# One reciprocal-square-root table function in place of Ln and Exp, in front of a kept Newton step

## The chip, the cores and the metric

The kernel runs on one core of one Trainium2 chip. The metric is device time in microseconds (us) of one execution. The core has a matrix engine (PE in the profile, with its weight loads as PEld), a vector engine (DVE), an activation engine (ACT), GpSimd (POOL), and SyncE (SP), which issues most DMA transfers. Each engine works through its own instructions in a fixed order and waits on semaphores for the others.

## The reference

Three stages stand behind each other: a linear attention with a root-mean-square norm, and two MLPs with different activations.

```
kv  = einsum('bhsd,bhse->bhde', k, v)
out = einsum('bhsd,bhde->bhse', q, kv)
rms = sqrt(mean(out * out, axis=-1) + 1e-06)
x   = out / rms * g_norm                      # 8 batches, 8 heads, 576 x 64 each
h = x @ w_in1;  g = where(h >= 1, h, where(h <= -1, 0, (h + 1)**2 / 4));  x = g @ w_out1
h = x @ w_in2;  g = max(h, 0)**2;                                         out = g @ w_out2
```

There are 4608 tokens, the model width is 512, and the hidden width of each MLP is 2048. Weights arrive as 64-bit floats and are read as pairs of 32-bit words.

## The kernel before, in words

Every fp32 product of the MLPs is made from three matmuls on pieces: each operand is split into a rounded upper piece (a CAST on ACT, line 217) and the remainder (a subtraction on DVE, lines 185, 230 and 807). The tokens are worked through in blocks of 512. Blocks of the first MLP are plain (`h_stage`, `g_stage`, `out_stage`, the matmuls of line 238); later work goes in pairs of blocks with fewer products (line 878).

The attention of batch 0 comes first, by four pairs of heads hp = 0 to 3 (`t_first`, `o_first`, `r_first`), with fillers on PE (`keep_warm`, matmuls on a tile of zeros, line 1157) between them. The attention of the other seven batches (`t_stage`, `o_stage`, `r_stage`) is spread as hooks over the steps of the block before. Beside the first attention the weights are narrowed and split (`split_w`: a Prelu on ACT in line 268, two DVE operations in lines 270 and 271, a CAST and a subtraction).

For one pair of heads the norm does this. PE multiplies q and kv into `po` (two halves of 288 columns), ACT squares each half into `y` (line 512) and scales it into `o` (line 209; DVE does the second half in line 211), PE averages the squares over a head with a matrix of ones into `pr` (line 534). Then comes the inverse root: ACT takes Ln of each half (line 535), Exp of both halves at once (line 537) and the square of the result into `t` (line 224, reached from line 538). DVE makes the Newton step: `newton` multiplies `t` by `pr` plus 1e-6 (line 519, once for each half), `norm` adds -3 and multiplies by `y` (line 522) and then by `o` (line 523). The result is split into the upper and lower piece of `x`, on which the first MLP's matmuls wait. In `r_stage` the same statements stand in lines 602, 604 and 606.

The eight PSUM banks are handed out in a ring during the first attention. So `pr` of pair 1 takes the bank of `pr` of pair 0, and has to wait until DVE's line 519 has read that; and a group of three fillers takes the bank of `pkv` of pair 2, and has to wait until DVE has copied that (line 219). A scheduler puts the instructions of each engine in order by its own estimates of their durations and by priorities; the program's text gives only dependencies and a rough order.

Of the kernel before, what the change touches and what calls it, by code (L numbers as in the profile page):

```python
# [10 lines left out]
F32 = mybir.dt.float32  # L11
F32R = mybir.dt.float32r
AF = mybir.ActivationFunctionType
ALU = mybir.AluOpType
I32 = mybir.dt.int32
BF16 = mybir.dt.bfloat16

LN_SCALE = 2.0**-44  # L20
LN2 = 0.6931471805599453

# [51 lines left out]
def linear_attention_rms_two_mlps(  # L78
# [12 lines left out]
    nc = tc.nc  # L91
# [3 lines left out]
    P = 128  # L95
# [17 lines left out]
    const = ctx.enter_context(tc.tile_pool(name="const", bufs=1))  # L113
# [73 lines left out]
    ident = ap2.tile([P, P], F32, tag="q", name="ident")  # L187
    ones = const.tile([P, P], F32R, name="ones")
    gvec = const.tile([P, 1], F32, name="gvec")
    lnb = const.tile([P, 1], F32, name="lnb")  # L190
    expb = const.tile([P, 1], F32, name="expb")
    halfb = const.tile([P, 1], F32, name="halfb")
    kv0 = wp.tile([P, NP, P], F32, tag=f"w1_{NF - 1}", name="kv0")
    rests = [const.tile([P, 2, 2, D], F32, name=f"rest{i}") for i in range(2)]
# [9 lines left out]
    def engine(op, phase):  # L204
        return engines[next(turns[op][min(phase, 2)])]
# [16 lines left out]
    def square(e, dst, src):  # L222
        if e is nc.scalar:
            e.activation(dst, src, AF.Square)  # L224
        else:
            e.tensor_tensor(dst, src, src, ALU.mult)

    def split(t, src, op, phase):
        hi = copy(engine(op + "_hi", phase), t[:, 0, :], src)
        lo = engine(op + "_lo", phase).tensor_tensor(  # L230
            t[:, 1, :], src, t[:, 0, :].bitcast(F32), ALU.subtract
        )
        return hi, lo
# [162 lines left out]
    def bank(b, name):  # L396

        pool, tag = next(banks) if b == 0 else (ps_t, "at")
        return pool.tile([P, TB], F32, tag=tag, name=name)

    def scratch(hp, kind):

        which, f = {"y": (0, 12), "o": (0, 8), "t": (1, 11), "qT": (1, 7)}[kind]
        return wp.tile([P, 2, U], F32, tag=f"w{which}_{f + hp}", name=f"{kind}_0_{hp}")
# [36 lines left out]
    def load_first():  # L441


        left = wp.tile([REM, 2, H, D], F32, tag="w0_7", name="kvr0")
        qr = wp.tile([REM, H, D], F32, tag="w1_6", name="qr0")
        for hp in range(NP):
            load_kv(0, hp)
            heads = slice(2 * hp, 2 * hp + 2)
            kvr[0, hp] = (left[:, 0, heads, :], left[:, 1, heads, :])
            pool, tag = (ep, "e") if hp == NP - 1 else (st, "st")  # L450
            t = pool.tile([P, TB], F32, tag=tag, name=f"q_0_{hp}")
            t = t.rearrange("p (c h d) -> p c h d", h=2, c=MR)
            rows = q[0, 2 * hp : 2 * hp + 2, :TB, :].rearrange("h (p c) d -> p c h d", p=P)
            nc.sync.dma_start(t, rows)
            qs[0, hp] = [t[:, c] for c in range(MR)] + [qr[:, heads, :]]
            if hp == 1:
                for f in range(2):
                    load_w(1, f, 0)
            if hp == 0:
                for d, src in ((left[:, 0], k), (left[:, 1], v), (qr, q)):  # L460
                    nc.scalar.dma_start(d, src[0, :, TB:, :].rearrange("h p d -> p h d"))
                for j in range(2):
                    nc.scalar.dma_start(
                        gvec[j * D : (j + 1) * D, :], g_norm.rearrange("(d o) -> d o", o=1)
                    )
# [52 lines left out]
    def newton(t, m):  # L518
        nc.vector.scalar_tensor_tensor(t, m, 1e-6, t, op0=ALU.add, op1=ALU.mult)  # L519

    def norm(t, y, o):
        nc.vector.scalar_tensor_tensor(t, t, -3.0, y, op0=ALU.add, op1=ALU.mult)  # L522
        nc.vector.tensor_tensor(t, o, t, ALU.mult)
# [3 lines left out]
    def r_first(hp):  # L527
        y, o = og.pop((0, hp))
        t = scratch(hp, "t")
        ms = []  # L530
        for half in range(2):
            ps = bank(0, f"pr_0_{hp}_{half}")
            m = ps[:, :U]
            nc.tensor.matmul(m, ones.bitcast(F32), y[:, half], start=True, stop=True)  # L534
            nc.scalar.activation(y[:, half], m, AF.Ln, bias=lnb, scale=LN_SCALE)
            ms.append(m)
        nc.scalar.activation(y, y, AF.Exp, bias=expb, scale=-0.5)
        square(engine("y", 0), t, y)
        for half in range(2):
            newton(t[:, half], ms[half])  # L540
        norm(t, y, o)
        n = TB // 2
        rem = xrem[0][:, hp, :].rearrange("p (h r) -> p h r", h=2)
        nc.gpsimd.tensor_copy(rem, t[:, :, n:])
        x = xs[1, 0][hp].rearrange("p a (h n) -> p a h n", h=2)
        marks.append(split(x, t[:, :, :n], "x", 0))
# [42 lines left out]
    def r_stage(b, hp):  # L589
        (y, o), _ = hl.pop((b, hp))  # L590
        if (b, hp) in WHOLE:
            products = [(ones.bitcast(F32), y)]
        else:
            products = [(ones, s2) for s2 in og.pop((b, hp))]
        ms = []
        for half in range(2):
            c = slice(half * U, (half + 1) * U)
            ps = bank(b, f"pr_{b}_{hp}_{half}")
            m = ps[:, :U]
            for n, (one, s2) in enumerate(products):  # L600
                nc.tensor.matmul(m, one, s2[:, c], start=n == 0, stop=n == len(products) - 1)  # L601
            nc.scalar.activation(y[:, c], m, AF.Ln, bias=lnb, scale=LN_SCALE)
            ms.append((c, m))
        nc.scalar.activation(y, y, AF.Exp, bias=expb, scale=-0.5)
        t = ap1.tile([P, S], F32, tag="wk2", name=f"t_{b}_{hp}")
        square(engine("y", b), t, y)
        for c, m in ms:
            newton(t[:, c], m)
        if b < LAST_B:
            norm(t, y, o)  # L610
            nc.gpsimd.tensor_copy(xrem[b][:, hp, :], t[:, TB:])
            split(xs[1, b][hp], t[:, :TB], "x", b)
            return
        xt = st.tile([P, TB], F32, tag="st", name=f"xt_{hp}")
        nc.vector.scalar_tensor_tensor(t, t, -3.0, y, op0=ALU.add, op1=ALU.mult)
        nc.vector.tensor_tensor(xt, o[:, :TB], t[:, :TB], ALU.mult)
        nc.vector.tensor_tensor(xrem[b][:, hp, :], o[:, TB:], t[:, TB:], ALU.mult)
        x_kept[hp] = xt
# [17 lines left out]
    def attention_first():  # L636

        slots = {}

        def at(s, f, *a):  # L640
            slots.setdefault(s, []).append((f, a))

        at(0, begin, 0)
        for hp in range(NP):
            at(6 * hp, kv_stage, 0, hp)
            at(6 * hp, t_first, hp)
            at(6 * hp + 8, o_first, hp)
            at(6 * hp + 13, r_first, hp)
        return slots

    def attention(b, base, every, order):

        slots = []
        for j, hp in enumerate(order):
            s = base + every * j
            turn.setdefault((b, hp), len(turn))
            if b == 1:
                slots += [(max(0, s - 7), load_kv, b, hp), (s, kv_stage, b, hp)]
            elif j % 2 == 0:
                two = order[j : j + 2]  # L660
                turn[b, two[1]] = len(turn)
                slots += [(max(0, s - 7), load_kv, b, i) for i in two]
                slots.append((s, kv_stage, b, *two))
            slots += [
                (max(0, s - 7), load_q, b, hp),
                (s, t_stage, b, hp),
                (s + 3, o_stage, b, hp, 0),
                (s + 4, o_stage, b, hp, 1),
            ]
            if j == 0:  # L670
                slots.append((s + 6, begin, b))
            slots.append((s + 6, r_stage, b, hp))
            if b == LAST_B:
                slots.append((s + 8, keep_x, b, hp))
        if b < LAST_B:
            slots.append((2 * NF * b, store_xrem, b))
        return slots
# [465 lines left out]
    for i, t in enumerate((7, 9, 11, 13, 15, 21, 23)):  # L1143
        hook(last + t, load_w2)

    nc.scalar.preload_act_table_set("natural_log_exp_and_others")
    load_first()
    for f, w in ((2, 0), (3, 0), (0, 1), (4, 0), (1, 1), (5, 0), (2, 1), (6, 0), (3, 1)):
        load_w(1, f, w)
# [18 lines left out]
        nc.gpsimd.memset(t, 0.0)  # L1168
    nc.gpsimd.memset(kv0, 0.0)
    nc.vector.tensor_scalar_mul(gvec, gvec, -0.5)  # L1170
    nc.vector.memset(lnb, LN_SCALE * 1e-6)
    nc.vector.memset(expb, -22.0 * LN2)
    nc.vector.memset(halfb, 0.5)

    kvw = ap1.tile([P, 2, P], F32, tag="hl1", name="kvw")
# [10 lines left out]
    for s in sorted(first):  # L1186
        for f, a in first[s]:
            if f in (o_first, r_first):
                with tc.high_priority():
                    f(*a)  # L1190
            else:
                f(*a)
# [102 lines left out]
```

## Time and profile before

| | us |
|---|---|
| median of 3 runs | 1556.57 (1556.27 to 1558.22) |
| the profiled execution's own time | 1556.74 |
| span of its instructions | 1554.7 |
| ACT busy in the span | 909.6 |
| DVE busy in the span | 1131.3 |

The profiled execution is 0.17 us above the median, and 2.04 us of it lie outside the span. The granted TensorE clock reads 1.00 over the span.

### The profile page before, as it was taken

To read this page: it belongs to the slowest core of one execution; us is meant where nothing else is said; L and a number is where in the kernel's file an instruction comes from. 1 tells how busy PE (TensorE), PEld (TensorE's weight loads), DVE (VectorE), ACT (ScalarE), POOL (GpSimd) and SP (SyncE) were. 2 spreads that over 40 slices of the span, in tenths; PEclk is the share of its full clock that TensorE was granted. 3 is DMA by queue.
4 is the path that set the end of the run, shared out by engine and by line. 5 is a ranking of instruction groups with operands and counts; after the bars stand their busy time and mean duration, and the time that the engine had idled before them with its cause. 6 is when DMAs were issued, how large, how long until landed. Compare 5 with 4: busy or idle time off the path is not lost.

```text
span 1554.7 us, 22267 instructions
## 1 busy us (share of the span) xinstructions
PE 1545.8 (99%) x7727; PEld 1283.3 (83%) x7729; DVE 1131.3 (73%) x2000; ACT 909.6 (59%) x1713; POOL 20.5 (1%) x38
## 2 busy tenths in 40 slices
PE   9999999999999999999999999999999999999999
PEld 5787888888888888888888888888888888888898
DVE  6986886877877776754587559778965596558666
ACT  5977766767666676664355346456644463446354
POOL 0000000000000000000000000000000000000000
PEclk9999999999999999999999999999999999999999
DMA  9666899996877967935676867696876676877796
GB/s 288 197 216 187 278 319 279 304 313 197 274 250 238 284 208 227 293 98 172 193 245 194 227 213 246 197 238 200 259 227 204 205 238 197 241 248 224 212 392 249
DMA packets 327519, 368.22 MB, mean 237 GB/s; under 512 B 196976, under 2 KB 222576, under 8 KB 327408
## 3 DMA queue, kind: packets, MB, share of 16 engines
q1 hardware_dynamic: 295360, 308.60, 66.4%
q10 hardware_dynamic: 32048, 58.20, 9.9%
q8 instruction: 61, 1.00, 0.3%
q14 instruction: 50, 0.41, 0.1%
HBM read 282.59 MB, written 84.15 MB: 236 GB/s over the span
## 4 chain that ended last, share of the span: by engine, by line
PE 97%; ACT 1%; DVE 1%; issue 0%; DVEq 0%; ACTq 0%
PE po L878 27%; PE ph L878 27%; PE acc L238 20%; PE ph L238 19%; PE pkv L479 1%; PE po L238 1%; PE pr L601 1%; PE pwarm L1157 1%; ACT raw L268 0%; ACT w L217 0%; PE pr L534 0%; DVE t L519 0%; DVE w L185 0%; PE po L511 0%; DVE t L522 0%; PE po L569 0%
## 5 line engine op out<-in xcount | busy, mean ns | idle before, releaser
L878 PE MATMUL ph<-x,ws 128*128 128x512 f32 (+1 forms) x2016 | 422.4, 371 | 0.0
L878 PEld LDWEIGHTS ph<-x,ws 128*128 128x128 f32 x2016 | 355.8, 188 | 65.6
L878 PE MATMUL po<-t,ws 128*128 128x512 f32 x1680 | 381.6, 389 | 0.0
L878 PEld LDWEIGHTS po<-t,ws 128*128 128x128 f32 x1680 | 315.3, 188 | 65.5
L238 PE MATMUL ph<-x,w 128*128 128x512 f32 x1344 | 329.4, 392 | 1.3 <-ACT w L217 0.6
L238 PEld LDWEIGHTS ph<-x,w 128*128 128x128 f32 x1344 | 248.7, 188 | 54.3 <-ACT w L217 1.5
L807 DVE TENSOR_TENSOR t<-g,t 128x512 fp32r<-128x512 f32 (+1 forms) x288 | 183.3, 641 | 92.2 <-ACT t L217 84.6
L217 ACT CAST t<-g 128x512 fp32r<-128x512 f32 (+1 forms) x288 | 166.5, 585 | 101.8 <-PE po L878 50.2
L238 PE MATMUL acc<-gs,w 128*128 128x512 f32 x696 | 173.0, 392 | 1.5 <-DVE u L707 1.5
L238 PE MATMUL acc<-gs,wt 128*128 128x512 f32 x648 | 157.9, 391 | 0.0
L238 PEld LDWEIGHTS acc<-gs,w 128*128 128x128 f32 x696 | 128.6, 188 | 27.8 <-DVE u L707 1.9
L949 ACT ACTIVATE g<-h 128x512 f32<-128x512 f32 (+1 forms) x120 | 70.7, 589 | 119.8 <-DVE h L938 119.8
L238 PEld LDWEIGHTS acc<-gs,wt 128*128 128x128 f32 x648 | 120.1, 188 | 24.3
L705 ACT ACTIVATE u<-ph,halfb 128x512 f32<-128x512 f32 x112 | 77.2, 690 | 91.5 <-PE ph L238 89.1
L938 DVE CUSTOM_DVE_ANT_0 h<-ph,e 128x512 f32<-128x512 f32 (+1 forms) x120 | 76.4, 638 | 64.8 <-PE ph L878 57.3
L707 DVE SCALAR_TENSOR_TENSOR u<-u,ph 128x512 f32<-128x512 f32 x112 | 76.3, 681 | 54.2 <-ACT u L224 53.8
L928 DVE TENSOR_TENSOR e<-ph,e 128x512 f32<-128x512 f32 (+1 forms) x96 | 61.1, 643 | 50.2 <-PE ph L878 49.6
L230 DVE TENSOR_TENSOR gs<-u,gs 128x512 fp32r<-128x512 f32 x112 | 76.8, 686 | 22.2 <-ACT gs L217 21.8
L217 ACT CAST gs<-u 128x512 fp32r<-128x512 f32 x112 | 69.7, 622 | 37.5 <-DVE u L707 34.7
L224 ACT ACTIVATE u<-u 128x512 f32<-128x512 f32 x112 | 70.8, 632 | 1.4 <-ACT u L705 0.5
L217 ACT CAST x<-xr 128x512 fp32r<-128x512 f32 (+1 forms) x84 | 49.0, 586 | 36.0 <-DVE xr L858 17.5
L807 DVE TENSOR_TENSOR x<-xr,x 128x512 fp32r<-128x512 f32 (+1 forms) x84 | 53.1, 637 | 7.3 <-ACT x L217 7.3
(134 smaller groups left out, 1494.5 us busy)
## 6 DMA issues: line engine op xcount, KB each, us to landing
ws<-wsd SPq DMA_DIRECT2D x336, 512.0 KB, 4.2
wsd<-s ACTq DMA_DIRECT2D x96, 512.0 KB, 4.7
wt<-wsd SPq DMA_DIRECT2D x54, 512.0 KB, 5.4
raw<-in_moe_w_in_dram SPq DMA_DIRECT2D x32, 512.0 KB, 5.8
raw<-in_moe_w_out_dram SPq DMA_DIRECT2D x32, 512.0 KB, 6.2
xr<-x1d SPq DMA_DIRECT2D x36, 256.0 KB, 4.9
out_dram<-ov SPq DMA_DIRECT2D x142, 64.0 KB, 3.5
wsd<-w SPq DMA_DIRECT2D x17, 512.0 KB, 5.0
```

Source lines behind the costliest of these rows:

```text
L217: return e.copy(dst, src)
L224: e.activation(dst, src, AF.Square)
L230: lo = engine(op + "_lo", phase).tensor_tensor(t[:, 1, :], src, t[:, 0, :].bitcast(F32), ALU.subtract)
L238: nc.tensor.matmul(dst, wt(a), xt(c), start=first and n == 0, stop=last and n == 2)
L479: nc.tensor.matmul(ps[s, d], lhs, rhs, start=c == 0, stop=c == MR)
L705: nc.scalar.activation(u, ps, AF.Relu, bias=halfb, scale=0.5)
L707: nc.vector.scalar_tensor_tensor(u, u, 1.0, ps, op0=ALU.min, op1=ALU.max)
L807: engine2(op + "_lo").tensor_tensor(t[:, 1, :], src, t[:, 0, :].bitcast(F32), ALU.subtract)
L878: nc.tensor.matmul(ps, wt(a), xt(c), start=first and n == 0 and i == 0, stop=last and n == len(lhs) - 1 and i == 2, skip_group_check=True,)
L928: nc.vector.tensor_tensor(e[i, p], bank, e[i, 1], ALU.add)
L938: nc.vector._custom_dve(TENSOR_ADD_SAT, out=h, in0=bank, in1=add, s0=float("inf"), s1=0.0)
L949: nc.scalar.activation(g, h, AF.Square)
```

## The change

The two Ln activations and the Exp of a pair become two activations with the function Abs_reciprocal_sqrt, which write `y` directly; the constant tiles for Ln and Exp go, one for 1e-6 comes, and the table set that is loaded at the start is another. The square, the Newton step and all that follows stay. There are 32 pairs, 4 in `r_first` and 28 in `r_stage`.

```
-LN_SCALE = 2.0**-44
-LN2 = 0.6931471805599453
...
-    lnb = const.tile([P, 1], F32, name="lnb")
-    expb = const.tile([P, 1], F32, name="expb")
+    epsb = const.tile([P, 1], F32, name="epsb")
...
-            nc.scalar.activation(y[:, half], m, AF.Ln, bias=lnb, scale=LN_SCALE)
+            nc.scalar.activation(y[:, half], m, AF.Abs_reciprocal_sqrt, bias=epsb)
             ms.append(m)
-        nc.scalar.activation(y, y, AF.Exp, bias=expb, scale=-0.5)
         square(engine("y", 0), t, y)
...
-            nc.scalar.activation(y[:, c], m, AF.Ln, bias=lnb, scale=LN_SCALE)
+            nc.scalar.activation(y[:, c], m, AF.Abs_reciprocal_sqrt, bias=epsb)
             ms.append((c, m))
-        nc.scalar.activation(y, y, AF.Exp, bias=expb, scale=-0.5)
...
-    nc.scalar.preload_act_table_set("natural_log_exp_and_others")
+    nc.scalar.preload_act_table_set("abs_reciprocal_sqrt_and_small")
...
-    nc.vector.memset(lnb, LN_SCALE * 1e-6)
-    nc.vector.memset(expb, -22.0 * LN2)
+    nc.vector.memset(epsb, 1e-6)
```

The scheduler answers with another order on ACT, DVE, PE and SP, from the first pair of heads on. Lines of the changed kernel are 7 to 11 smaller than those before; the names with numbers are tiles, and the first number behind `y`, `o`, `t`, `pr`, `po` and `pkv` is the pair of heads.

ACT, first attention, from the mean squares of pair 0 to the square into `t` of pair 0, before:

```order
L535 ACTIVATE y_0_282<-pr_0_0_333,lnb 128x288
L268 ACTIVATE raw_0_0_151<-raw_0_0_151 128x512
L535 ACTIVATE y_0_282<-pr_0_1_336,lnb 128x288
L537 ACTIVATE y_0_282<-y_0_282,expb 128x576
L512 ACTIVATE y_1_348<-po_1_0_350 128x288
L209 ACTIVATE o_1_349<-po_1_0_350,gvec 128x288
L512 ACTIVATE y_1_348<-po_1_1_354 128x288
L224 ACTIVATE t_0_332<-y_0_282 128x576
L217 CAST w_0_0_300<-d_0_0_297 128x2x256
L268 ACTIVATE raw_0_1_153<-raw_0_1_153 128x512
```

ACT at the same place, of the changed kernel:

```order
L527 ACTIVATE y_0_280<-pr_0_0_331,epsb 128x288
L260 ACTIVATE raw_0_0_150<-raw_0_0_150 128x512
L527 ACTIVATE y_0_280<-pr_0_1_334,epsb 128x288
L216 ACTIVATE t_0_330<-y_0_280 128x576
L260 ACTIVATE raw_0_1_152<-raw_0_1_152 128x512
L504 ACTIVATE y_1_345<-po_1_0_347 128x288
L201 ACTIVATE o_1_346<-po_1_0_347,gvec 128x288
L504 ACTIVATE y_1_345<-po_1_1_351 128x288
L209 CAST w_0_0_298<-d_0_0_295 128x2x256
```

The Exp is gone, the square into `t` of pair 0 has moved ahead of the three instructions of pair 1, and so has the Prelu on `raw_0_1`, whose input comes by DMA.

DVE, first attention, from the Newton step of pair 0 to the first copies of pair 2 (`kv` and `qT`, which PE reads for `po` of pair 2), before:

```order
L519 SCALAR_TENSOR_TENSOR t_0_332<-pr_0_0_333,t_0_332 128x288
L519 SCALAR_TENSOR_TENSOR t_0_332<-pr_0_1_336,t_0_332 128x288
L185 TENSOR_TENSOR w_0_0_300<-d_0_0_297,w_0_0_300 128x2x256
L522 SCALAR_TENSOR_TENSOR t_0_332<-t_0_332,y_0_282 128x576
L271 SCALAR_TENSOR_TENSOR d_0_1_363<-raw_0_1_153,d_0_1_363 128x512
L523 TENSOR_TENSOR t_0_332<-o_0_283,t_0_332 128x576
L219 COPY kv_126<-pkv_2_303 64x64 x2
L219 COPY qT_2_316<-pt_2_0_317 128x288
L519 SCALAR_TENSOR_TENSOR t_1_393<-pr_1_0_394,t_1_393 128x288
```

DVE, of the changed kernel, from the Newton step of pair 1 (that of pair 0 stands seven rows ahead of it, directly behind line 263 on `d_0_0`):

```order
L511 SCALAR_TENSOR_TENSOR t_1_390<-pr_1_0_391,t_1_390 128x288
L511 SCALAR_TENSOR_TENSOR t_1_390<-pr_1_1_394,t_1_390 128x288
L222 TENSOR_TENSOR x_0_0_215<-t_0_330,x_0_0_215 128x512
L514 SCALAR_TENSOR_TENSOR t_1_390<-t_1_390,y_1_345 128x576
L211 COPY kv_125<-pkv_2_301 64x64
L515 TENSOR_TENSOR t_1_390<-o_1_346,t_1_390 128x576
L211 COPY kv_125<-pkv_2_301 64x64
L211 COPY qT_2_314<-pt_2_0_315 128x288
L211 COPY qT_2_314<-pt_2_1_320 128x288
L222 TENSOR_TENSOR x_0_1_216<-t_1_390,x_0_1_216 128x512
```

The copies of pair 2 stood ahead of the Newton step of pair 1 and now stand behind it. On PE, one of the four fillers ahead of `pr` of pair 1 stands behind it now, `po` of both halves of pair 2 stands together now, behind five fillers, and so does `pr` of pair 2; before, `pr` of its second half stood behind the first two matmuls of the MLP. POOL's order is the same, and SP's too through the first attention; later some loads of weights, q and k change places on SP by a few rows.

## Rows read from the trace of the kernel before

**Rows 1.** The page, busy time of each engine in the span.
```profile
PE 1545.8 (99%) x7727; PEld 1283.3 (83%) x7729; DVE 1131.3 (73%) x2000; ACT 909.6 (59%) x1713; POOL 20.5 (1%) x38
```
**Rows 2.** Waits of PE, whole span: us in total, times, longest.
```profile
PE acc L238 <- DVE u L707: 1.5, 1, 1.5
...
PE pr L534 <- DVE t L519: 0.9, 1, 0.9
PE ph L238 <- ACT w L217: 0.6, 2, 0.4
PE ph L238 <- DVE kv L219: 0.4, 1, 0.4
```
**Rows 3.** Busy time in two stretches: PE, PEld, DVE, ACT, POOL; clock, DMA, GB/s.
```profile
40.00:60.00 20.00, 18.05 (x91) 13.22 (x90) 18.76 (x35) 19.66 (x40) 0.00 (x0) 1.00 0.95 274
60.00:1550.00 1490.00, 1489.82 (x7422) 1247.07 (x7421) 1084.52 (x1899) 867.03 (x1630) 16.83 (x24) 1.00 0.76 236
```
**Rows 4.** Timeline of PE: start us, us, instruction, idle before it.
```profile
1.19 4.73 PE L1157 MATMUL pwarm<-warm 128*128 128x512 bf16 x11 [1.19 <-DVE warm L1152]
...
17.82 1.24 PE L534 MATMUL pr<-y,ones 128*128 128x288 f32 x4 [0.91 <-DVE t L519]
...
32.30 13.03 PE L238 MATMUL ph<-x,w 128*128 128x512 f32 x56 [0.28 <-DVE t L519]
...
49.00 3.33 PE L238 MATMUL ph<-x,w 128*128 128x512 f32 x12 [0.44 <-ACT w L217]
53.84 0.97 PE L238 MATMUL acc<-gs,w 128*128 128x512 f32 x3 [1.51 <-DVE u L707]
...
57.33 4.27 PE L238 MATMUL acc<-gs,w 128*128 128x512 f32 x17
```
**Rows 5.** Instructions of ACT by form: count, busy us, mean ns, idle before.
```profile
L604 ACT ACTIVATE wk<-wk,expb 128x576 f32<-128x576 f32 x28 | 22.0, 785 | 0.3
...
L535 ACT ACTIVATE y<-pr,lnb 128x288 f32<-128x288 f32 x8 | 3.9, 501 | 3.7 <-PE pr L534 3.7
```
**Rows 6.** Timeline of ACT, start and first attention.
```profile
0.73 1.28 ACT L1146 ACT_TABLE_LOAD   x1 [0.73 <-PEq L1273]
...
14.43 0.78 ACT L537 ACTIVATE y<-y,expb 128x576 f32<-128x576 f32 x1
...
16.58 0.69 ACT L224 ACTIVATE t<-y 128x576 f32<-128x576 f32 x1
17.16 0.63 ACT L217 CAST w<-d 128x512 fp32r<-128x512 f32 x1
17.66 0.69 ACT L268 ACTIVATE raw<-raw 128x512 f32<-128x512 f32 x1
...
20.82 0.68 ACT L224 ACTIVATE t<-y 128x576 f32<-128x576 f32 x1
...
31.07 0.69 ACT L224 ACTIVATE t<-y 128x576 f32<-128x576 f32 x1
```
**Rows 7.** Timeline of DVE, first attention and the steps behind it.
```profile
15.34 0.42 DVE L270 TENSOR_SCALAR d<-raw 128x512 int32<-128x512 int32 x1
...
17.31 0.82 DVE L519 SCALAR_TENSOR_TENSOR t<-pr,t 128x288 f32<-128x288 f32 x2
...
19.92 0.75 DVE L523 TENSOR_TENSOR t<-o,t 128x576 f32<-128x576 f32 x1
20.59 0.45 DVE L219 COPY kv<-pkv 64x64 f32<-64x64 f32 x2
...
39.34 0.68 DVE L230 TENSOR_TENSOR x<-t,x 128x512 fp32r<-128x512 f32 x1
...
53.11 0.68 DVE L707 SCALAR_TENSOR_TENSOR u<-u,ph 128x512 f32<-128x512 f32 x1
```
**Rows 8.** Timeline of SP's queue: the issue of the first weight loads.
```profile
7.35 0.93 SPq L250 DMA_DIRECT2D raw<-in_moe_w_in_dram  x2
```
**Rows 9.** The weight tiles raw up to 62 us: time from issue to landing.
```profile
DMA to landing us min/median/max: 4.4/8.1/11.2
```

## The prediction

> **What bounds the kernel now.** I read the page's engine totals first: PE is busy for 1545.8 of 1554.7 us, ACT for 909.6, DVE for 1131.3 [rows 1]. A gain on ACT alone is therefore worth something only where PE waits for ACT or for what hangs on it. The second view, the list of PE's waits, says how little that is: apart from its first start, PE waits in five places of the whole program, for 1.5, 0.9, 0.6 and 0.4 us [rows 2] and the 0.28 that stands at 32.30 [rows 4], 3.7 us together. The third, busy time by stretches, says where: from 60 to 1550 us PE is busy for 1489.82 of 1490 us, while ACT has 867.03 us of work there, so that 28 of the 32 removed Exps come out of time in which ACT has room; from 40 to 60 us ACT (19.66 of 20) and DVE (18.76) are full and PE is not (18.05) [rows 3]. The fourth, PE's timeline, gives the places: 0.91 us at 16.9 before `pr` of pair 1, 0.28 at 32.0, 0.44 at 48.6, and 1.51 at 52.3 before the first `acc` [rows 4]. Behind that PE hardly waits again. So the change is worth what it moves the first 58 us, and the rest shifts with it.
>
> **What goes.** Per pair of heads, one Exp of 0.78 us, 28 of them in the later batches [rows 5, 6]. A queued instruction starts about 0.1 us before the one ahead ends (the square at 16.58 lasts 0.69, the CAST behind it starts at 17.16 [rows 6]), so the Exp holds ACT's queue for 0.68 us, 4 x 0.68 = 2.7 us in the first attention. The 28 others lie beside PE work; that cover goes only if ACT becomes full again, and the change makes it emptier.
>
> **What comes.** The new function has no row. The nearest is the Ln it replaces, with the same operands (PSUM source, a tile as bias, 128x288): 0.501 us [rows 5]. I take that, so 0. Below it could lie 0.4, if it cost as little as 0.1 less per half; above it the Exp's 0.78 on twice the columns, 0.28 more per half, 0.56 per pair. With the upper end four pairs lose 2.2 us on ACT, nearly all that the Exp gives.
>
> **What moves, place by place.** I laid the rows of the new order behind each other from 13 us on, each with the duration of the same instruction before, less the overlap of 0.1 us; I give the points that decide.
>
> At 14 us: the second root of pair 0 ends near 14.4, where the Exp starts now [rows 6], and the square into `t` follows at once, ahead of pair 1: 14.4 instead of 16.58. DVE's two Newton instructions move up into the place that line 270 has now, 15.34 instead of 17.31 [rows 6, 7]. That frees the bank for which `pr` of pair 1 waits. The next limit is pair 1's own squares. Their way is longer by the Prelu on `raw_0_1`, which now stands ahead of them and holds ACT until about 15.8; the squares then end at 16.2 and 16.9. PE, with three fillers in place of four after `po`, reaches `pr` at 16.6 and goes on without a wait: 1.2 us before the 17.82 of now [rows 4]. The square into `t` of pair 1 comes at 18.4 instead of 20.82 [rows 6].
>
> At 20 us the new order gives some back. The copies of `kv` of pair 2 run at 20.59 now [rows 7]; in the new order they stand behind pair 1's Newton pair (19.1 to 19.85), a split (0.60) and lines 522 and 523 (0.67 each, as from 19.92 to 20.59), and end at 22.2 with their own 0.45 [rows 7]. PE, done with the transposes at 20.0 and with three fillers at 20.6, meets a filler that needs this bank: a new wait of about 1.6 us, with nothing on PE to hide it, since all that is queued behind it waits too: `po` and `pr` of pair 2, and all of pair 3. Behind it `po` of pair 2 runs whole, so both halves of `pr` come at 26.6 and 27.2, and the square into `t` of pair 2 at 29.0 instead of 31.07 [rows 6]. PE has done by 31.3 what it has done by 32.30 now, the small wait there included [rows 4]: 1.0 us ahead, while ACT and DVE are 2 us ahead.
>
> From 31 to 51 us: the last split of `x` comes on DVE at 37.3 instead of 39.34 [rows 7]. PE is covered until then by matmuls on the first three pieces, as now. Then DVE and ACT are full [rows 3]. DVE goes through 24 rows from there to line 707 of step 2, the one that frees the bank of the first `acc`; 7 of them line 270 at 0.34 us, 17 others at 0.60, and three waits for CASTs of 0.5 together, that is 13.1 us from 37.9 on, so line 707 starts at 51.0 instead of 53.11 [rows 7], and `acc` at 51.7 instead of 53.84 [rows 4]. PE gets there at 51.6: of its lead of 1.0 it first loses some at the weights of step 6 (`ph`, at 49.00 now, [rows 4]), whose upper piece I place at 48.4 and whose lower piece at 49.3; the wait of 1.51 is turned into two of 0.8 and 0.5.
>
> From there to 57.7 the order differs by a few matmuls; counted by matmuls done, 0.1 to 0.2 us more is gained. Sum: -2.1 and -0.1, **2.2 us earlier**, and PE has no later wait to give it back. On SP nothing is moved past another within the first attention; the loads that change places later are covered by PE's run from 60 to 1550 us [rows 3], and if one should come late, that is a new stall of case E. 1556.74 - 2.2 = 1554.5 for an execution like the profiled one, which is 0.17 above the median: **1554.4 us**.
>
> A rule of the Trainium skill speaks against the change. The trace shows the load of a table once, 1.28 us at the start [rows 6], and the order of the changed kernel holds one too. The Trainium skill, "ScalarE: Activation LUTs", section "Table sets: the hidden batching unit", says that a function outside the active set needs a load of its set first, and prices a switch at about 2.66 us. If Square, Prelu or Relu were not in the new set, that would be an estimate of 8 switches on the way of the first four pairs, 21 us by that page; the single load in the order speaks against it.
>
> **Rivals.** (B) The gain does not arrive, about 1556.6. It would be so if the stretch from 31 to 57 us, where DVE is full, began no earlier: if the new function costs the upper bound, or the wait at 20.6 us is 2 us longer than I place it. For it: DVE's 18.76 of 20, and that one place gives back 1.6 us already. Against it: ACT's chain of pair 2 comes out 2 us early even with that wait.
>
> (C) More than forecast, about 1553.0: the new wait at 20.6 is short, the lower piece of step 6's weights is in time, and PE keeps 3.5 us. The waits that exist add up to 3.7, and the 12 matmuls at 49.00 take 0.6 more than at the pace of the 56 at 32.30, 0.23 us each [rows 4]; 4.3 less, 1552.3, is the floor.
>
> (D) Slower than before, about 1558.7: the Prelu on `raw_0_1` now stands ahead of pair 1 on ACT, and waits for a DMA. Its load is the second of the two issued from 7.35, done by 8.3 [rows 8]; these loads land 4.4 to 11.2 us after issue [rows 9]. Each microsecond past 15.2 delays all behind it; from 17.4 on the gain is gone, and at 8.3 + 11.2 = 19.5 it costs 4.3 - 2.2 = 2.1 us. Against it: line 270 of now reads this tile at 15.34 [rows 7], so it had landed.
>
> (E) The loads of tables come back, in ACT's chain of the first attention: two a pair, by the row of the load [rows 6] 8 x 1.28 - 2.2 = 8 us more, 1564.6; or some load on SP holds up a block. The order's single load speaks against the first, the work that covers PE against the second.
>
> The clock is no case of its own: the eleven fillers from 1.19 us on take 0.43 us each, 512 columns at the lower of the two levels (1.2 GHz), while after the wait of 1.51 us at 52.3 the 17 matmuls at 57.33 take 0.25 each, the upper one [rows 4]; the new wait is as long as that one.
>
> **Chances.** Forecast 0.60, own range 1553.3 to 1555.6; B 0.15; C 0.15; D 0.06; E, with any other new stall in the reordered steps, 0.04. What this measurement tells from no change is about 0.2%, 3.1 us, so from 1553.46 down it is faster and from 1559.68 up slower. Faster: C and 0.05 of the forecast, 0.20. Slower: E and half of D, 0.07. The rest, 0.73, is within. The range goes from 1552.6, just under C, to 1557.8, over B and the milder part of D.
>
> **What would show it.** In the changed profile: line 537 gone and one table load; the new function at 0.50 us; the square into `t` of pair 0 near 14.4 and of pair 2 near 29; PE's wait before `pr` of pair 1 gone, a wait of 1 to 2 us at a filler near 20.6 in its place; `acc` first at 51 to 52.5; no wait of PE between 60 and 1550 us; ACT busy for some 25 us less in all. A wait of PE after 60 us, or an `acc` at 53.8 or later, would make the forecast wrong; so would a Prelu that waits for its DMA at 15 us.

## The result and the profile after

| | before | after |
|---|---|---|
| median of 6 runs, us | 1556.79 (1556.27 to 1558.81) | 1565.95 (1564.18 to 1568.39) |
| after / before, 95% interval | | 1.0057 (1.0045 to 1.0070) |
| profiled execution: own time, span, us | 1556.74, 1554.7 | 1568.35, 1566.6 |

The change makes the kernel 0.57% slower, some 9 us. The forecast was 1554.4 us, and the range ended at 1557.8. One execution of the thirteenth run below (2274.56 us, mean granted clock 0.635) and one of the kernel before (1937.68 us, 0.746) are left out of every comparison.

In the changed kernel the lines are 7 to 11 lower: the new function is line 527 (535 before) and 593 (602), a matmul of the MLPs 230 (238), a CAST 209 (217), `u` 697 (707), Newton 511, 514 and 515 (519, 522, 523), `qf` and `qT` 549 and 551 (558, 560), `wf` 333 (341).

The engine totals, which answer to [rows 1]:

```profile
PE 1550.2 (99%) x7729; PEld 1285.1 (82%) x7729; DVE 1129.9 (72%) x1999; ACT 888.8 (57%) x1681; POOL 14.6 (1%) x38
```

ACT has lost 20.8 us of work, and PE has gained 4.4 with the same matmuls (two records of them are missing in the trace before). Then the waits of PE, against [rows 2]: engine, what waits, what it waits for, us in total, times, longest.

```profile
PE po L230 <- ACT qT L209: 3.4, 3, 2.5
PE ph L230 <- DVE u L697: 3.1, 2, 1.6
PE pwarm L1147 <- DVE kv L211: 1.5, 1, 1.5
PE ph L230 <- ACT w L209: 1.3, 1, 1.3
...
PE pr L592 <- ACT wk L201: 1.0, 1, 1.0
PE pkv L471 <- DMA v<-in_v_dram: 0.8, 2, 0.6
```

PE's timeline, against [rows 4], puts them in their places:

```profile
23.31 0.80 PE L1147 MATMUL pwarm<-warm 128*128 128x512 bf16 x2 [1.51 <-DVE kv L211]
...
51.18 3.37 PE L230 MATMUL ph<-x,w 128*128 128x512 f32 x12 [1.31 <-ACT w L209]
54.48 1.91 PE L230 MATMUL acc<-gs,w 128*128 128x512 f32 x7
...
120.82 0.40 PE L592 MATMUL pr<-s,ones 128*128 128x288 f32 x1 [0.97 <-ACT wk L201]
132.14 3.02 PE L230 MATMUL ph<-x,w 128*128 128x512 f32 x12 [1.61 <-DVE u L697]
...
209.93 0.40 PE L230 MATMUL po<-qT,kvbd 128*128 128x288 f32 x1 [0.45 <-ACT qT L209]
321.46 3.01 PE L230 MATMUL ph<-x,w 128*128 128x512 f32 x12 [1.53 <-DVE u L697]
500.80 0.40 PE L230 MATMUL po<-qT,kvbd 128*128 128x288 f32 x1 [0.47 <-ACT qT L209]
556.18 0.61 PE L230 MATMUL po<-qT,kvbd 128*128 128x288 f32 x1 [2.51 <-ACT qT L209]
```

Six waits stand where the kernel before had one of 0.18 us [rows 3]: 0.97 + 1.61 + 0.45 + 1.53 + 0.47 + 2.51 = 7.5 us. The busy times by stretches say the same, and show the clock (the column behind POOL):

```profile
22.00:24.00 2.00, 0.69 (x3) 0.30 (x3) 1.94 (x6) 0.62 (x1) 0.24 (x1) 0.89 1.11 359
24.00:26.00 2.00, 2.00 (x6) 1.12 (x5) 1.31 (x3) 0.80 (x2) 0.00 (x0) 0.50 1.04 373
26.00:28.00 2.00, 2.00 (x25) 1.25 (x23) 0.85 (x3) 1.88 (x4) 0.00 (x0) 0.76 1.05 384
...
60.00:1550.00 1490.00, 1482.19 (x7327) 1236.53 (x7326) 1077.62 (x1884) 845.64 (x1594) 11.22 (x24) 1.00 0.77 235
556.00:562.00 6.00, 5.82 (x21) 4.94 (x22) 3.45 (x7) 3.85 (x11) 0.00 (x0) 0.72 0.86 225
```

From 60 to 1550 us PE is busy 7.6 us less than before. At the waits that end at 23.31 and 556.18 us the granted clock is 0.89, 0.50 and 0.76 in three stretches and 0.72 in the last, down at the lower of its two levels (1.2 GHz of 2.4) for all or part of them. Worked out from these rows, that costs PE (0.11 + 0.50 + 0.24) x 2 + 0.28 x 6 = 3.4 us, most of its 4.4 us more of busy time. Where the last 1.0 comes from is not shown; it need not be the clock, since in the profile of the tenth run below PE is busy for 1548.0 us, 2.2 more than before, with a clock of 1.00 from 60 to 1550 us. The account of the two profiled spans closes: 7.4 us more of waits behind 60 us and 4.4 more of busy time make 11.8 of the 11.9 us. The waits of the first 60 us, first start included, add up to 4.8 us in both.

The six executions fit this. The two with a mean granted clock of 1.000 took 1564.2 and 1564.3 us, 7.5 above the kernel before, as much as the six waits; the other four, at 0.998 and 0.999, took 1566.0 to 1568.4.

Where the waits come from is read on DVE's timeline. This is the step ahead of the longest:

```profile
546.59 0.69 DVE L333 TENSOR_TENSOR wf<-wf 128x512 f32<-128x512 f32 x1 [3.36 <-DMA wf<-wsd]
547.20 0.68 DVE L697 SCALAR_TENSOR_TENSOR u<-u,ph 128x512 f32<-128x512 f32 x1
...
549.39 0.81 DVE L511 SCALAR_TENSOR_TENSOR t<-pr,t 128x288 f32<-128x288 f32 x2
...
554.16 0.77 DVE L549 STREAM_TRANSPOSE qf<-q 128x576 f32<-128x576 f32 x1
```

DVE stands 3.36 us for the transfer of `wf`, a weight tile that is being prepared for later steps. Behind it in the queue stand `u` (an activation of an MLP), a Newton step and `qf` (a transposed q); ACT makes `qT` from `qf`, and PE waits 2.51 us for `qT`. In the kernel before, this Newton step (537.46 us) and `qf` (542.87) were done before DVE came to `wf` (558.16).

### The profile page after: what moved, and what is told of

It is laid out like the page before. It is cut to its first block, busy times and chain, and to the rows that moved or that the text cites. A ratio compares the mean times of both kernels' runs of the same rounds, so it can differ in the third digit from the quotient of the medians.

```text
span 1566.6 us, 22236 instructions
## 1 busy us (share of the span) xinstructions
PE 1550.2 (99%) x7729; PEld 1285.1 (82%) x7729; DVE 1129.9 (72%) x1999; ACT 888.8 (57%) x1681; POOL 14.6 (1%) x38
## 4 chain that ended last, share of the span: by engine, by line
PE 66%; DMA 1%; DVE 1%; ACT 0%; issue 0%; SPq 0%; DVEq 0%
PE po L868 27%; PE ph L868 27%; PE acc L230 6%; PE ph L230 5%; PE po L230 0%; DMA wf<-wsd 0%; DMA x1d<-ev 0%; PE pkv L471 0%; PE pr L592 0%; ACT qT L209 0%; DVE gs L222 0%; DVE u L697 0%; ACT s L209 0%; DVE t L515 0%; DVE t L511 0%
```

## The experiments

Theory (order): the list scheduler, given 32 instructions less, wrote another order for every engine; some instructions that wait for a transfer, or weights that have time, now stand in front of steps that PE needs. The order moved 164 of PE's 7385 instructions, 357 of ACT's 1811, 419 of DVE's 1999 and 49 of SP's 940. Rival (function): the reciprocal square root, its table, or the Newton step behind it costs the time. The addresses came in as a second rival after the first four runs.

Where an order is pinned, each engine's instructions get edges that fix their order and nothing else, from a table:

```diff
+ORDER = {"PE": ..., "Activation": ..., "DVE": ..., "SP": ..., "Pool": ...}
...
+        for a, b in zip(order, order[1:]):
+            tc.add_manual_dep(b, a.name, ..., reason="order")
...
         linear_attention_rms_two_mlps(tc, *args)
+        pin_order(tc)
```

Ratios are to the kernel before, in runs on the same chip, with 95% intervals.

### Order or function: four runs

The first puts a do-nothing operation where the Exp stood, so that the scheduler writes the old order (in both places):

```diff
+        nc.scalar.activation(y, y, AF.Identity, bias=zerob, scale=1.0)
```

> The kernel after with one more ACT operation (Identity, y to y, at both places where Exp stood). All work of the kernel after is in it, and every engine has its instructions in the order of the kernel before. Order theory (the loss of the kernel after is the new order that the scheduler gave all engines when the Exp went): within 1.5 us of the kernel before, about 1556.7 us, and the PE waits of the kernel after behind 60 us (120.8, 132.1, 209.9, 321.5, 556.2 us, some 7.5 us together) are gone. Function theory (the reciprocal square root itself, its table or what it leaves to the Newton step costs the time): as the kernel after, 1564 to 1568 us, with the same waits.

Measured: 1557.70 us, ratio 1.0000 (0.9991 to 1.0009). From 60 to 1550 us PE has one wait of 0.18 and one of 0.24 and is as busy as before [rows 3] (PE alone; then clock, DMA, GB/s):

```profile
60.00:1550.00 1490.00, 1489.58 (x7414) 1.00 0.77 236
```

The second takes the Exp out of the kernel before (in both places), which gives the new order without the new function:

```diff
-        nc.scalar.activation(y, y, AF.Exp, bias=expb, scale=-0.5)
```

> The kernel before with the Exp left out (the Newton step is given the logarithm, so the output is not the reference's): Ln stays, no new function, and the order of all engines is that of the kernel after. Order theory: as the kernel after, 1564 to 1568 us, with PE waits near 121, 132, 210, 321, 500 and 556 us. Function theory: no slower than the kernel before, 1552 to 1557 us.

Measured: 1566.61 us, 1.0059 (1.0046 to 1.0071), as the kernel after. Its waits of PE:

```profile
PE po L238 <- ACT qT L217: 5.0, 3, 2.8
PE ph L238 <- DVE u L705: 2.3, 2, 1.6
```

They stand at 118.8, 130.1, 210.3, 322.1, 502.1 and 556.7 us, the places of the kernel after. These two runs settle it: the function is innocent, the order is not. Both keep two constants, and with them the addresses of the kernel before, so the second rival does not touch this reading.

The third is the new function in the old order, pinned; the fourth pins the new order up to 61.7 us and the old one behind it.

> The kernel after, with the order of every engine's instructions pinned to that of the kernel before without the Exp. Order theory: the gain that the prediction saw in the first 60 us and nothing lost behind it, 1553.5 to 1557 us, no PE wait above 0.5 us behind 60 us, the filler's wait of 1.5 us at 22 us gone and the old one at 52 us back. Function theory: 1564 to 1568 us. A third reading (in before's order the gain of the first stage is taken back at the next wait anyway, since the pace of the start is set by transfers) gives 1556 to 1557 us, the same as before.

> The kernel after with the order pinned: its own order up to the second projection of the block at 61.7 us, and from there the order of the kernel before. Theory: the first attention alone costs at most 2.5 us (0.5 us that PE is behind at 58 us, and up to 1.7 us where the clock falls behind the filler's wait), so 1556 to 1559 us; the rest of the loss (5 to 9 us) is in the order behind 61.7 us. Rival: what is lost was laid in the first attention, with the later waits as its echo: 1563 us or more.

Measured: 1560.12 us, 1.0015 (1.0006 to 1.0023), and 1560.82, 1.0018 (1.0009 to 1.0027). The fourth is 0.7 us above the third, with intervals that overlap, so the new order of the first attention loses little; the great part lies behind it. But both miss their ranges. The fourth lies 1.8 us above its own, and the third fits none of its readings: old order, less work, and 2.5 us slower. In its profile PE waits 1.29 us for the first `v`, until 6.65, and 1.00 us for `qT` at 642. Two causes, taken up in turn.

### The addresses: four runs

The change also drops a constant. Two of 32 bytes a partition (`lnb`, `expb`) become one (`epsb`), and all tiles allocated behind them lie 32 bytes lower. In the kernel before 1069 of the 1071 places in SBUF that DMAs read or write start at 0 of 256 bytes, after the change at 224.

```diff
 # fifth and sixth run: a spare behind epsb, read by nothing
+    spare = const.tile([P, 1], F32, name="spare")
 # seventh: the kernel before, constants in one tile
-    lnb = const.tile([P, 1], F32, name="lnb")
-    expb = const.tile([P, 1], F32, name="expb")
+    bias2 = const.tile([P, 2], F32, name="bias2")
+    lnb, expb = bias2[:, :1], bias2[:, 1:]
 # eighth: the kernel before
+    spare = const.tile([P, 1], F32, name="spare")
```

> The kernel after with one spare constant that nothing reads, in the place where the second constant of the logarithm and Exp stood. The kernel before had two constants of 32 bytes a partition there, the kernel after one, so that every tile behind lies 32 bytes lower: all 1069 ends of DMAs in SBUF start at 0 of 256 bytes before and at 224 of 256 after. The spare puts them back to 0; the order of all engines is that of the kernel after. Address theory (the shift lengthens transfers: the first v lands so that PE starts its second pkv at 11.2 us in place of 10.0, and the pinned kernel without Exp lost 2.5 us against the kernel before): 1.5 to 3 us under the kernel after, 1562 to 1565 us, first v and k transfers at 5.4 us median in place of 6.3. Order theory alone: 1564 to 1568 us.

> The kernel after with the order of the kernel before (as in the third run) and the spare constant, so that nothing is left of the change but the function in place of Ln and Exp. Address theory: the 2.5 us of the third run come back, 1555 to 1557.5 us; what is left under the kernel before is what the Exp itself cost, 0 to 1.5 us. Rival (with the Exp gone in a fixed order, work of ACT comes earlier into transfers and waits there): 1559 to 1561 us, as the third run.

> The kernel before with its two constants as the two columns of one tile: all work, Ln, Exp and the order of every engine as before, and only the addresses moved, 32 bytes lower (224 of 256). Address theory: 2 to 3 us slower than the kernel before, 1559 to 1561 us, with the first v and k transfers at 6.3 us and more. Rival: no difference, 1556 to 1558 us.

> The kernel before with one spare constant more: all addresses 32 bytes higher (32 of 256). Two forms of the address theory: if any start off a multiple of 64 bytes costs, 1559 to 1561 us as with 224; if the cost lies in the 32 bytes left in front of a boundary of 256, hardly anything, 1556 to 1558.5 us. The Trainium skill's DMA: Bandwidth & Descriptors, How a descriptor splits into AXI transactions, has the second form: by its rule 512 bytes from 224 take 23 beats of 32 bytes in place of 16, from 32 they take 17.

Measured: 1565.03 us, 1.0052 (1.0039 to 1.0065); 1558.23, 1.0006 (0.9997 to 1.0015); 1559.46, 1.0013 (1.0004 to 1.0022); 1558.58, 1.0008 (0.9999 to 1.0017). The seventh run is the clean one: all work and the order as before, only the addresses moved, 2 us slower. The issues of the first 12 us show it, with the median us to landing at the end of a row. First of the kernel before (0 of 256), then of the seventh run (224), then of the eighth (32):

```profile
k<-in_k_dram SPq DMA_DIRECT2D x4, 256.0 KB, 5.4
v<-in_v_dram SPq DMA_DIRECT2D x3, 256.0 KB, 5.3
```

```profile
k<-in_k_dram SPq DMA_DIRECT2D x3, 256.0 KB, 6.2
v<-in_v_dram SPq DMA_DIRECT2D x3, 256.0 KB, 6.3
```

```profile
k<-in_k_dram SPq DMA_DIRECT2D x3, 256.0 KB, 6.4
v<-in_v_dram SPq DMA_DIRECT2D x3, 256.0 KB, 6.5
```

A first load takes some 1 us longer off the old place, at 32 as at 224; the kernel after has 6.3 and 6.4. All sixteen profiles divide this way: 5.2 to 5.8 us for these two rows in the eleven at 0, 6.2 to 6.9 in the five off it.

PE's timeline shows how 1 us of a load becomes 2.8 us in the profile of the seventh run; first the kernel before, then the seventh:

```profile
5.84 0.69 PE L479 MATMUL pkv<-v,k 128*64 128x64 f32 x16
6.46 1.47 PE L1157 MATMUL pwarm<-warm 128*128 128x512 bf16 x6
```

```profile
7.06 1.12 PE L479 MATMUL pkv<-v,k 128*64 128x64 f32 x16 [1.00 <-DMA v<-in_v_dram]
8.12 2.66 PE L1157 MATMUL pwarm<-warm 128*128 128x512 bf16 x6
```

PE starts 1.2 us later, and what follows the wait runs at the lower clock level, the six fillers at 0.44 us each in place of 0.25: 1.6 us more. So `pkv` of pair 1 comes at 12.87 in place of 10.03, and the span is 2.8 us longer. In the eighth run's profile the clock does not add to it, and `pkv` of pair 1 comes at 11.27.

The Trainium skill's "DMA: Bandwidth & Descriptors", "How a descriptor splits into AXI transactions", says that a read that starts off a boundary of 256 bytes is fetched from the boundary below it. These loads write to the places that moved, and the Trainium skill tells there of reads alone; carried over to them, as an estimate, its rule would make a start at 32 cost hardly anything and one at 224 much. The loads do not bear this out: both are equally late.

Whether the whole time is equally late at 32 the eighth run leaves open, since its interval reaches from no change to the seventh's. In the new order the spare is worth 0.8 us by the ratios (1.0052 against 1.0057), which the intervals do not tell from nothing: the address is the small part.

### The one wait that was left

The sixth run has old order and old addresses, and its median is still 1.1 us above the kernel before, though its interval reaches below 1. What is plain is a new wait: PE waits 1.51 us for `qT` at 641.9. ACT's timeline shows why (ACTq rows are DMA issues in ACT's queue):

```profile
624.39 0.34 ACTq L170 DMA_DIRECT2D x1d<-ev  x1
...
630.17 0.35 ACTq L170 DMA_DIRECT2D x1d<-ev  x1
630.56 0.62 ACT L210 CAST gs<-u 128x512 fp32r<-128x512 f32 x1 [3.07 <-DMA x1d<-ev]
```

The scheduler hands out eight semaphores to the program's 1071 DMAs, and a DMA waits until the last holder of its semaphore has landed. Without the Exp, in the same order, 48 of them got another one. (In the kernel after it is 359, and what this costs there is not separated from the order.) The fourth of these writes now has the same one as the first, issued at 624.39, and ACT stood until that had landed. The eleventh run moves this one issue behind the next seven operations of ACT (the expectation counts eight):

```
ACT's order, sixth run:     x1d(2) x1d(3) gs s x u wk u wk x ...
ACT's order, eleventh run:  x1d(2) gs s x u wk u wk x1d(3) x ...
```

> The sixth run (function alone, order and addresses of the kernel before) with one instruction moved: the issue of the fourth write of x1d on ACT's queue, at 630 us, goes behind the eighth operation after it. In the sixth run this write got the semaphore of the first one of the four (in the kernel before that of an older load), so ACT stood 3.07 us until the first had landed, and PE waited 1.51 and 0.39 us for qT at 642 us. Semaphore theory: these waits go, 1.5 to 1.9 us less than the sixth run, 1556 to 1557 us, which is where the kernel before lies or up to 1 us below it. Rival (the transfers of that stretch are slower by themselves): 1558 to 1559 us, as the sixth run.

Measured: 1557.00 us, 0.9998 (0.9989 to 1.0006). The wait at 642 is gone, and the kernel is level with the one before; by the intervals alone the sixth and the eleventh are not told apart. So with order, addresses and this semaphore held, the removal of all 32 Exps is worth between 1.7 us and -0.9: not measurable. (The move also changed the semaphore of that write, so the two ways of avoiding the wait are not told apart.) No version was found that beats the kernel before.

### The order wait by wait

The tenth run puts the old order in front and the new one behind 61.7 us; the ninth and twelfth take the new order whole and move single DVE instructions back. All three have the spare.

```
DVE, near 20 us (ninth and twelfth)
  after: t t x t kv t kv qT qT x      moved: kv kv qT t t qT x t t x
DVE, near 113, 128, 317, 544 us (ninth)
  after: u gs qf qT                   moved: u qf gs qT
  after: w d t d t u w x              moved: w u d t d t w x
  after: d wf s s u s                 moved: d u wf s s s
  after: wf u s s s d t t gs t t      moved: u t t t t wf s s s d gs
```

> The kernel after with the spare constant, with the order of the kernel before up to the second projection of the block at 61.7 us and its own order behind it. If the loss lies behind 61.7 us, as the fourth run has it from the other side: 1562 to 1565 us, with the PE waits at 120, 131, 320 and 554 us, and no fall of the clock at 24 us. If it was laid in the first attention: 1557 to 1559 us.

> The kernel after with the spare constant and its own order, with only the four copies of kv_2 and qT_2 on DVE put ahead of the Newton step of pair 1, so that PE does not wait for them at 22.3 us. Clock theory (the wait of 1.5 us lets the granted clock fall to 0.5 at 24 us, and the matmuls behind it take double): 1.52 us of wait and 1.2 us of slow matmuls go, so 1561 to 1563 us, and the granted clock is 1.0 in each stretch of 2 us from 16 to 30 us. Rival (the fall comes from elsewhere, or the time is waited for a little later): 1563.5 to 1565.5 us.

> The kernel after with the spare constant and its own order on all engines, but for 12 of DVE's 1999 instructions that are put earlier, at the five PE waits of the spare kernel's profile that they end: the copies of kv_2 and qT_2 ahead of the Newton step of pair 1 (wait of 1.52 us at 22.3), the transpose qf ahead of a gs (0.98 at 119.8), one u ahead of the weights of other blocks (1.61 at 131.1), one u ahead of wf, which waits for its transfer (0.82 at 319.6), and a u and the Newton step of a pair ahead of another wf (1.87 at 553.8). Order theory, wait by wait: the five waits go, 6.8 us less, and the clock no longer falls at 24 us (1.2 us) and 560 us: 1556 to 1559 us. Rival (the order is late as a whole, so that a wait removed comes back at the next hand-over): 1562 us or more.

Measured: the tenth 1565.04 us, 1.0047 (1.0035 to 1.0060), in its profile waits of 0.97, 1.59, 0.89, 1.00 and 1.87 us behind 60 us and a clock of 1.00 at 24: the loss lies behind 61.7 us. The twelfth 1565.26, 1.0050 (1.0036 to 1.0064), a miss: it lies where the rival had it. In its profile the wait of 1.52 us at 22 has become one of 0.74 there and one of 0.59 at 27, the clock stays at 1.00 from 22 to 28, and the span is 1561.2, but the median is not below the fifth run's 1565.03. What its slower executions lost is not seen. The ninth 1564.34, 1.0037 (1.0024 to 1.0049), a miss against 1556 to 1559. Its five executions fall apart: 1560.1 and 1560.8, and three at 1564.3 to 1565.1 with a lower mean clock (0.998). The profile is of the 1560.8. Three of the moves did what was expected (131, 320 and 554 us have no wait above 0.22 any more); the move of `qf` changed nothing, since PE's own order put 22 matmuls of `acc` in front of its `po`; and one old wait of 0.42 had grown:

```profile
PE po L231 <- ACT qT L210: 2.5, 1, 2.5
PE ph L231 <- ACT w L210: 1.4, 1, 1.4
```

It stands at 208.6 and is the same thing again: DVE waits 3.45 us for a `wf`, with `x`, `gs` and `qf` behind it. The thirteenth run moves that `wf` as well, and the fourteenth does the opposite: it takes the kernel before and puts this one `wf` where the new order has it.

```
DVE, thirteenth (with the ninth's moves)   after: wf x gs qf     moved: x gs qf wf
DVE, fourteenth (kernel before)            before: x u qf wf gs  moved: wf x u qf gs
```

> The ninth run (the kernel after with the spare constant and 12 DVE instructions put earlier) with one more move: wf of 205 us, which stood 3.45 us waiting for its transfer, goes behind the x, gs and qf that stood behind it. That was the one large PE wait left in the profile of the ninth run behind 130 us (2.50 us at 208.6, 0.42 in the run without the moves). Order theory, wait by wait: the wait goes, 1556.5 us of span in a profile with the clock at 1.000, 1557.5 to 1560 us as median; and if the lower clock of three of the ninth run's five executions (0.998, 1564 to 1565 us) came behind that wait, none lies below 0.999. Rival: another wait grows in its place, or the clock falls all the same, 1562 us or more.

> The kernel before, Ln, Exp, addresses and all, with one of its 14,000 instructions moved: DVE's wf of 202.5 us goes ahead of the x, u and qf of 200.1 to 202.0 us, where the order of the kernel after has it. Order theory: DVE stands from 200.1 until the transfer has landed at 202.5, x, u, qf and qT come 2.4 to 3 us later, PE waits 1 to 2.5 us for qT near 205 us: 1558.5 to 1560 us, more where the clock falls behind it. Rival (a single such move is taken up by the slack of the engines, and it takes the whole reorder to lose time): 1556.5 to 1557.8 us.

Measured: the thirteenth 1559.91 us, 1.0016 (1.0007 to 1.0025), the executions compared between 1558.2 and 1561.6, with a mean clock of 0.999 or 1.000. Its longest waits:

```profile
PE ph L231 <- ACT w L210: 1.4, 1, 1.4
PE pwarm L1148 <- DVE warm L1143: 1.2, 1, 1.2
PE pr L593 <- ACT wk L202: 1.0, 1, 1.0
```

So 13 of 1999 DVE instructions bring back some 5 of the 8 us that the new order costs (1.0052 to 1.0016); the rest, with the two PE waits above of 1.4 and 1.0 us, was not pursued. The fourteenth 1558.83, 1.0010 (1.0001 to 1.0019): one instruction moved in the kernel before costs 1.8 us, by the interval 0.2 to 3.0. DVE and, in the second fence, PE show how:

```profile
202.94 0.69 DVE L341 TENSOR_TENSOR wf<-wf 128x512 f32<-128x512 f32 x1 [2.25 <-DMA wf<-wsd]
203.55 0.68 DVE L230 TENSOR_TENSOR x<-t,x 128x512 fp32r<-128x512 f32 x1
204.16 0.68 DVE L707 SCALAR_TENSOR_TENSOR u<-u,ph 128x512 f32<-128x512 f32 x1
204.75 0.77 DVE L558 STREAM_TRANSPOSE qf<-q 128x576 f32<-128x576 f32 x1
```

```profile
206.28 0.40 PE L238 MATMUL po<-qT,kvbd 128*128 128x288 f32 x1 [1.24 <-ACT qT L217]
```

The transfer lands at its usual time; only now `x`, `u` and `qf` stand behind it, and 1.24 us reach PE, which never makes them up. (This profile is of the slowest execution, 1560.11 us, and has one more new wait, 0.74 us at 386.88 for DVE's `s2lo`, which is not traced to the move.)

## Why the prediction was wrong

**The step that failed.** "Behind that PE hardly waits again. So the change is worth what it moves the first 58 us, and the rest shifts with it", and with it "PE has no later wait to give it back" and, of the loads, that PE's run from 60 to 1550 us covers them [rows 3]. A PE without waits was read as slack on the engines that feed it. It was none: it said that in the old order every operand came in time, some by little. Six new waits, 7.5 us, came where 0 was put. Case E named them ("any other new stall in the reordered steps") with 0.04. That its 1564.6 us lies near the measured time is chance: it was worked out for eight loads of tables. Two of the prediction's three signs of a wrong forecast came, waits of PE behind 60 us and an `acc` later than 53.8. A small misreading stands beside it: the waits of the kernel before are in six places, not five, since the 0.6 us for `w` are two [rows 2], 0.44 at 48.6 and the 0.18 behind 60 us.

**The clock.** "The clock is no case of its own" failed too. It rested on one wait of 1.51 us that had cost no clock [rows 4]. In the kernel after a wait of 1.51 was followed by a granted clock of 0.50, one of 2.51 by 0.72, together some 3.4 us of PE's time.

**The constant.** That a constant went, and every address with it, the prediction did not look at. It costs 2 us in the old order (1.0013, 1.0004 to 1.0022); in the new order its 0.8 us are not told from nothing.

**The gain.** The first attention went nearly as written, where neither addresses nor clock disturb it. The function takes 0.50 us as assumed:

```profile
L593 ACT ACTIVATE wk<-pr,epsb 128x288 f32<-128x288 f32 x56 | 26.6, 497 | 8.6 <-PE pr L592 8.6
L527 ACT ACTIVATE y<-pr,epsb 128x288 f32<-128x288 f32 x8 | 4.0, 501 | 2.0 <-PE pr L526 2.0
```

In the fifth run the square of pair 0 starts at 14.55 (14.4 forecast), `pr` of pair 1 at 16.66 (16.6), the square of pair 1 at 18.36 (18.4), and the filler waits 1.52 us (1.6). In the second run, with the old addresses and no fall of the clock at 24 us, PE goes on like this:

```profile
31.30 13.80 PE L238 MATMUL ph<-x,w 128*128 128x512 f32 x59
...
49.09 3.37 PE L238 MATMUL ph<-x,w 128*128 128x512 f32 x12 [1.45 <-ACT w L217]
52.39 1.88 PE L238 MATMUL acc<-gs,w 128*128 128x512 f32 x7
```

31.3 was forecast for the first row, and 51.7 for `acc`: the gain there is 1.45 us in place of 2.1, because the weights of step 6 let PE go on at 49.09, where the prediction had 48.4: one wait of 1.45 in place of two of 0.8 and 0.5. In the kernel after even that does not show: its `acc` comes at 54.48, since PE starts `pkv` of pair 1 at 11.18 in place of 10.03 and the clock falls at 24. And most of the gain belonged to the new order, not to the Exp: in the old order the square of pair 0 stays behind pair 1's squares, which wait for PE, and the time of the Exp turns into idle time of ACT, 1.21 us at 15.97 in the eleventh run where it was 0.40. Some 0.5 us of PE's time is left of it there: `pr` of pair 1 starts at 18.19 (17.82 before), the first `acc` at 53.67 (53.84). The third and the sixth run show the same step, 0.6 us; in the whole time it is not measurable.

**The rivals.** B's time (no gain) is what the kernel has in the old order, though not for B's reason: neither did the function cost the upper bound, nor was the wait at 20.6 us longer than placed. D did not happen: ACT's Prelu on `raw_0_1` follows the row ahead of it without idle time, at 16.18. Of E the tables are excluded: the trace has one load, 1.28 us, as before [rows 6], so the set holds the Squares and Prelus too, and the rule that the prediction took from the Trainium skill's "ScalarE: Activation LUTs", "Table sets: the hidden batching unit", has nothing to act on.

## What to carry to other kernels

An engine at 100% in one order of a scheduler says nothing of the margin in the next one: take an instruction out, and look where the new order puts those that wait for a transfer, on the in-order queues that feed the bound engine. Tell the change from its order by a stand-in that keeps the order (a do-nothing operation) and by the order without the change; two runs did it here. Hold the addresses, too: a spare constant is enough.

## What the runs showed of the hardware

- One in-order instruction that waits for a transfer is enough: 2.25 us of DVE's time at 202 us became 1.24 us of PE's and 1.8 us (0.2 to 3.0) of the kernel's.
- A DMA issue in ACT's queue holds ACT's arithmetic: 3.07 us at 627 us, until an earlier write on the same semaphore had landed.
- 32 bytes of address made the first loads of k and v 1 us longer, in either direction (5.3 to 5.4 us against 6.2 to 6.5; over all sixteen profiles 5.2 to 5.8 against 6.2 to 6.9).
- The granted clock falls at some waits of PE of 1.5 us and more and not at others; each of the two falls of the kernel after cost PE some 1.7 us. It fell at the waits of 1.51 us at 23.3 and 2.51 at 556 (after), 1.51 at 23.7 (fourth run), 1.52 at 22.3 and 1.87 at 553.8 (fifth run) and 2.77 at 210 (second run); it stayed at 1.00 with those of 1.51 at 22.7 (second run), 1.87 at 553.9 (tenth run), 2.50 at 208.6 (ninth run's profile) and 1.51 at 53.8 (before). What decides it stays open.
